# Retention and two mixture layers on one core: the first load of turned queries and keys as one transfer or as two

## The chip, the cores and the metric

The kernel runs on one core of one Trainium2 chip. The metric is the device time of one execution in microseconds, as the median of several runs. Besides these runs there is one profiled execution; all rows of the trace come from it.

## What is computed

Three stages follow one another. The first is a retention (a linear attention with a decaying state) over 2 batches, 8 heads, 768 positions and 64 numbers a head; the second is a dense layer of 512 to 2048 to 512 with a leaky rectifier; the third sends each of the 1536 tokens to one of 8 experts.

```python
def _attn_ref(q, k, v):                      # 2, 8, 768, 64
    gamma = 1.0 - 2.0 ** (-5.0 - np.arange(H))
    for t in range(S):
        state = gamma * state + np.einsum('bhd,bhe->bhde', k[:, :, t], v[:, :, t])
        y[:, :, t] = scale * np.einsum('bhd,bhde->bhe', q[:, :, t], state)

def _moe_ref(x, w_in, w_out):                # 1536 x 512, 512 x 2048, 2048 x 512
    h = x @ w_in
    return np.maximum(0.01 * h, h) @ w_out

def _moe2_ref(x, w_gate, w1, w2, capacity):  # 8 experts, 512 x 1024 and 1024 x 512
    expert_idx = np.argmax(x @ w_gate, axis=1)
    ...
    h = np.maximum(np.einsum('ecd,edf->ecf', disp, w1), 0.0)
    y = np.einsum('ecf,efd->ecd', h, w2)
    ...
```

## The kernel before

The retention is done in chunks of 128 positions, six to a batch, so twelve chunks, named 0 to b. The host lays each chunk out as 128 rows of 2048 numbers: 512 of turned queries (head dimension on the partitions, two heads one above the other, so four pairs of heads beside each other), 512 of turned keys in the same layout, 512 of keys and 512 of values as they are. One load, `q` and the chunk, takes the first 1024 numbers of every row, and another, `k` and the chunk, the last 1024. Each is 512 KB: 128 rows of 4 KB.

All loads go through one function, `issue` (L148), on SyncE's queue, in the order of the list `LOADS` (L35): q0, k0, q1, w00, k1, q2, k2, q3 and so on. The first six go into tiles named `early`, the later ones into tiles named `land`. After load 0 the decay masks of the retention are loaded (`cst`, columns from `C_D`, 512 KB), and after load 1 the factors of queries and keys (`cst`, columns from `C_GQ`, 286 KB). The rest of the constants (206 KB) and the small `wg_sb` follow after all loads that can be issued at once.

The order of the engines' work in the front part is written out by hand in the list `FRONT` (L40). What begins it is `S.0 am.00 am.01 M.0 ks.0 D.0 xh.0 st.0 xl.0 S.1 qs.1 Y.1 am.10 am.11 ...`:

- S (L183, matmuls of L190) is the scores of a chunk: eight products, four pairs of heads by two heads, of turned keys and turned queries, two of them for each pair. An fp32 product stands as two MATMUL rows in the trace, so S.0 is 16 rows. Its loop takes the pairs in order.
- am (L212, DVE) multiplies the scores of one half of the heads by the decay mask in `cst`.
- M (L256, PE) multiplies the masked scores by the values, which come with load `k`.
- ks (L198, DVE) multiplies the keys by factors in `cst`; D (L228, PE) sums keys and values into the state; st (ACT) copies the state.
- xh (L265, ACT) and xl (L269, DVE) write the chunk's output as a high and a low part. qs (L207, DVE) and Y (L245, PE) bring in the state of earlier chunks. Chunk 0 has no qs and no Y.
- c1 to c4 and A1, A2 split the weights of the dense layer into a high and a low part (L291 to L310, on DVE and ACT).

Ahead of S.0, PE does nine matmuls with zeros (L1024) and one that clears the state (L217), and behind S.0 27 small ones with zeros (L1076). They need no load.

Of the kernel before, what the change touches and what calls it, by code (L numbers as in the profile page):

```python
# [59 lines left out]
def retention_moe_moe_kernel(ctx: ExitStack, tc: tile.TileContext, qkv, wb, wc, wg, const, out, cap):  # L60
    nc = tc.nc
# [86 lines left out]
    def issue():  # L148
        while issued[0] < len(items):
            n = issued[0]  # L150
            if n >= EARLY + LAND and items[n - LAND] not in done:
                return
            key = items[n]
            issued[0] += 1
            pool, tag = (early_p, "early") if n < EARLY else (land_p, "land")
            t = pool.tile([P, 1024], U32 if key[0] == "w" else F32, tag=tag, name=tag)
            if key[0] == "w":
                src = wb[key[1], :, key[2] * 1024:(key[2] + 1) * 1024]
            elif key[0] == "u":
                src = wc[key[1] // PF // slabs, key[1] % PF]  # L160
            else:
                o = 0 if key[0] == "q" else 1024
                src = qkv[key[1] // NCH, key[1] % NCH, :, o:o + 1024]
            nc.sync.dma_start(out=t, in_=src)
            if n in (0, 1):
                first_const.pop(0)()
            landed[key] = t

    def used(key):
        done.add(key)  # L170
        issue()
# [818 lines left out]
    def out_tiles():  # L990
        return [c_p.tile([P, DM], F32, tag="og", name="og", bufs=4) for _ in range(BT)]
# [23 lines left out]
    with tc.manual_schedule():  # L1015
# [10 lines left out]
        first_const.append(lambda: load_const(C_D, C_D + 1024))  # L1026
        first_const.append(lambda: load_const(C_GQ, C_ID))
        issue()
        load_const(C_ID, NC)
        nc.sync.dma_start(out=wg_sb, in_=wg)  # L1030
# [29 lines left out]
        for n in names:  # L1060
            n, c = n.split(".")
# [4 lines left out]
        for n in names:  # L1066
            n, c = n.split(".")
# [112 lines left out]
        for t in range(BT):  # L1180
# [14 lines left out]
            out=xr0[0][:, 0, :], out_offset=None, in_=x2d,  # L1195
# [36 lines left out]
        for s in range(NS):  # L1232
            o = out_tiles()
            n, base = every[s // slabs], (s % slabs) * BW
# [76 lines left out]
```

## Time and profile before

| | us |
|---|---|
| runs without the profiler, median of 3 | 527.96 |
| lowest and highest of them | 527.80, 528.04 |
| profiled execution, its own time | 526.96 |
| its span, first to last instruction | 525.1 |
| PE busy in the span | 509.6 |

The profiled execution is 1.0 us below the median of the runs. Time in the rows is counted from the start of the span. PE is the matmul engine, PEld its weight loads, DVE, ACT and POOL the vector, scalar and general engines, SPq the sequencer of SyncE, which issues the loads. A timeline's line gives start, duration, engine, line of the kernel, operation, written and read tiles, how many instructions were merged (x16), and in brackets the idle time ahead of it with what ended that.

### The profile page before, as it was taken

The page shows a single profiled execution, that of the slowest core. Times are in us where ns is not written, and L with a number is a line of the kernel's source. Part 1 is how long each engine was busy: PE and PEld are TensorE (multiplying, and loading weights), DVE is VectorE, ACT ScalarE, POOL GpSimd, SP SyncE. Part 2 cuts the span into 40 slices and gives each one's busy share as a digit, 9 for nine tenths or more (in the row PEclk, how much of TensorE's full clock was granted, in tenths as well). Part 3 has the DMA queues.
Part 4 walks back from the last instruction along what each step waited for, and adds up shares of the span by engine and source line. Part 5 has one row for each costly group of instructions (what it writes and reads, how often), then busy time and mean ns, then how long its engine had stood idle before and what let it go on. Part 6 is the DMA issues. An engine that isn't in the chain of part 4 may idle for free.

```text
span 525.1 us, 9022 instructions
## 1 busy us (share of the span) xinstructions
PE 509.6 (97%) x3328; PEld 459.9 (88%) x3330; DVE 338.7 (64%) x670; ACT 253.2 (48%) x573; POOL 50.1 (10%) x75
## 2 busy tenths in 40 slices
PE   8899999999999999999999999999979999999994
PEld 5888989999999999999999999789779899999893
DVE  3999994279779848974742445667534466676560
ACT  2886964365555534432423224346433266676440
POOL 0000000000000000000100107334010031220101
PEclk9999999999999999999999999999979999999998
DMA  8987672022315702220200108589445099993001
GB/s 308 398 282 241 229 248 102 1 81 81 101 42 142 249 30 80 81 80 1 81 32 29 61 1 296 168 277 318 160 149 206 7 335 361 330 371 119 24 10 44
DMA packets 24940, 80.79 MB, mean 154 GB/s; under 512 B 3706, under 2 KB 3834, under 8 KB 24864
## 3 DMA queue, kind: packets, MB, share of 16 engines
q1 hardware_dynamic: 21312, 70.26, 38.4%
q0 software_dynamic: 3552, 9.58, 5.2%
q8 instruction: 40, 0.66, 0.5%
q14 instruction: 36, 0.29, 0.2%
HBM read 72.35 MB, written 9.96 MB: 157 GB/s over the span
## 4 chain that ended last, share of the span: by engine, by line
PE 68%; DMA 24%; DVE 3%; issue 2%; ACT 1%; POOL 0%; SPq 0%; POOLq 0%; ACTq 0%; DVEq 0%
PE ps_h L363 25%; PE ps_y L414 16%; DMA out<-og,gix 12%; DMA xr<-x2d,gix 8%; PE ps_a L414 7%; PE ps_h L826 5%; PE ps_y L878 5%; PE ps_a L256 2%; PE ps_a L190 2%; PE ps_a L245 1%; DMA xpre<-wc,wix 1%; DMA early<-qkv 1%; PE ps_a L463 1%; DMA land<-qkv 1%; PE ps_h L228 1%
## 5 line engine op out<-in xcount | busy, mean ns | idle before, releaser
L370 ACT ACTIVATE hs<-ps_h 128x384 f32<-128x384 f32 x64 | 31.4, 490 | 97.1 <-PE ps_h L363 97.1
L375 DVE SCALAR_TENSOR_TENSOR hs<-hs 128x384 f32<-128x384 f32 x64 | 35.6, 556 | 65.7 <-ACT hs L370 65.5
L363 PE MATMUL ps_h<-xh,hi 128*128 128x384 f32 x256 | 56.3, 341 | 0.0
L414 PE MATMUL ps_y<-hi,gh 128*128 128x512 f32 x138 | 56.3, 408 | 0.0
L363 PE MATMUL ps_h<-xh,lo 128*128 128x384 f32 x256 | 55.5, 338 | 0.0
L363 PE MATMUL ps_h<-xl,hi 128*128 128x384 f32 x256 | 55.5, 338 | 0.0
L379 ACT ACTIVATE gh<-hs 128x384 fp32r<-128x384 f32 x64 | 33.7, 526 | 43.2 <-DVE hs L375 43.2
L414 PE MATMUL ps_y<-hi,gl 128*128 128x512 f32 x138 | 53.9, 391 | 0.0
L414 PE MATMUL ps_y<-lo,gh 128*128 128x512 f32 x138 | 53.8, 390 | 0.0
L363 PEld LDWEIGHTS ps_h<-xh,hi 128*128 128x128 f32 x256 | 46.0, 188 | 4.8
L385 DVE TENSOR_TENSOR gl<-hs,gh 128x384 fp32r<-128x384 f32 x64 | 35.6, 556 | 21.3 <-ACT gh L379 21.3
L363 PEld LDWEIGHTS ps_h<-xl,hi 128*128 128x128 f32 x256 | 45.9, 187 | 0.0
L363 PEld LDWEIGHTS ps_h<-xh,lo 128*128 128x128 f32 x256 | 45.9, 187 | 0.0
L878 PE MATMUL ps_y<-hi,gh 128*128 128x512 f32 x104 | 41.1, 395 | 0.0
L878 PE MATMUL ps_y<-hi,gl 128*128 128x512 f32 x104 | 40.8, 392 | 0.0
L878 PE MATMUL ps_y<-lo,gh 128*128 128x512 f32 x104 | 40.8, 392 | 0.0
L869 DVE SCALAR_TENSOR_TENSOR gl<-ps_h,gh 128x256 fp32r<-128x256 f32 (+2 forms) x42 | 16.6, 395 | 33.4 <-ACT gh L868 33.4
L849 DVE TENSOR_TENSOR lo<-xland,hi 128x1024 fp32r<-128x1024 f32 (+1 forms) x32 | 33.5, 1056 | 7.2 <-ACT hi L848 7.1
L868 ACT ACTIVATE gh<-ps_h 128x256 fp32r<-128x256 f32 (+2 forms) x42 | 15.3, 364 | 40.5 <-PE ps_h L826 25.4
L849 DVE TENSOR_TENSOR lo<-land,hi 128x1024 fp32r<-128x1024 f32 (+1 forms) x30 | 31.0, 1043 | 5.0 <-ACT hi L848 5.0
L414 PEld LDWEIGHTS ps_y<-hi,gl 128*128 128x128 f32 x138 | 25.9, 188 | 5.6
L414 PEld LDWEIGHTS ps_y<-hi,gh 128*128 128x128 f32 x138 | 25.9, 188 | 4.1 <-issue 0.3
(201 smaller groups left out, 1011.3 us busy)
## 6 DMA issues: line engine op xcount, KB each, us to landing
land<-wc SPq DMA_DIRECT2D x32, 512.0 KB, 6.9
xland<-wc SPq DMA_DIRECT2D x32, 512.0 KB, 5.1
land<-wb SPq DMA_DIRECT2D x31, 512.0 KB, 4.9
land<-qkv SPq DMA_DIRECT2D x19, 512.0 KB, 5.3
out<-zero SPq DMA_DIRECT2D x12, 256.0 KB, 6.0
x2d<-rows SPq DMA_DIRECT2D x12, 256.0 KB, 2.1
early<-qkv SPq DMA_DIRECT2D x5, 512.0 KB, 7.3
cst<-cst_in SPq DMA_DIRECT2D x1, 512.0 KB, 5.6
```

The lines of the kernel that those rows point to most:

```text
L190: nc.tensor.matmul(out=at["s", c][h2][:, a, :], lhsT=kT[r, a, :], rhs=qT[r, a, :], start=True, stop=True)
L363: nc.tensor.matmul(out=h_ps, lhsT=w[i][:, dc * P:(dc + 1) * P], rhs=x[j][:, dc, :], start=(n == 0), stop=(n == 3 * KD - 1))
L370: nc.scalar.activation(out=hs, in_=gt[u][0], func=ACTF.Copy)
L375: nc.vector.scalar_tensor_tensor(out=hs, in0=hs, scalar=0.01, in1=hs, op0=ALU.mult, op1=ALU.max)
L379: nc.scalar.activation(out=gh, in_=gt[u][0], func=ACTF.Copy)
L385: nc.vector.tensor_tensor(out=gl, in0=hs, in1=gh.bitcast(F32), op=ALU.subtract)
L414: nc.tensor.matmul(out=yb[ti][t], lhsT=gt[u][i][:, t * P:(t + 1) * P], rhs=w[j][:, 512:1024], start=(f == fs[0] and n == 0), stop=(f == fs ...
L826: r = nc.tensor.matmul(out=hp, lhsT=w[i][:, dc * P:(dc + 1) * P], rhs=(h, l)[j][:, dc, 0:cls * P], start=(n == 0), stop=(n == 3 * KD - 1))
L849: nc.vector.tensor_tensor(out=lo[:, o], in0=src[:, o], in1=hi[:, o].bitcast(F32), op=ALU.subtract)
L868: nc.scalar.activation(out=gh, in_=hp, func=ACTF.Relu)
L869: nc.vector.scalar_tensor_tensor(out=gl, in0=hp, scalar=0.0, in1=gh.bitcast(F32), op0=ALU.max, op1=ALU.subtract)
L878: nc.tensor.matmul(out=yps[t], lhsT=gg[i][:, t * P:(t + 1) * P], rhs=w[j][:, 512:1024], start=(k == 0 and n == 0), stop=(k == PF - 1 and n ...
```

## The change

Load 0 (q0) is issued as two transfers in place of one. Tile and source are seen as 128 rows of two halves (queries and keys) of 512 numbers; the first transfer takes the first 256 numbers of both halves, which are pairs 0 and 1 of queries and keys, the second the last 256, pairs 2 and 3. Each moves 256 KB in pieces of 1 KB, where the one before moved 512 KB in pieces of 4 KB. Everything else stands as it was; the masks are issued behind the second transfer.

```diff
@@ -161,7 +161,12 @@
             else:
                 o = 0 if key[0] == "q" else 1024
                 src = qkv[key[1] // NCH, key[1] % NCH, :, o:o + 1024]
-            nc.sync.dma_start(out=t, in_=src)
+            if n == 0:
+                by = [x.rearrange("p (m w) -> p m w", m=2) for x in (t, src)]
+                for o in (slice(0, 256), slice(256, 512)):
+                    nc.sync.dma_start(out=by[0][:, :, o], in_=by[1][:, :, o])
+            else:
+                nc.sync.dma_start(out=t, in_=src)
             if n in (0, 1):
                 first_const.pop(0)()
             landed[key] = t
```

## Rows read from the trace of the kernel before

**Rows 1.** The page: busy time by engine, and the chain that ended last.
```profile
PE 509.6 (97%) x3328; PEld 459.9 (88%) x3330; DVE 338.7 (64%) x670; ACT 253.2 (48%) x573; POOL 50.1 (10%) x75
...
PE 68%; DMA 24%; DVE 3%; issue 2%; ACT 1%; POOL 0%; SPq 0%; POOLq 0%; ACTq 0%; DVEq 0%
```

**Rows 2.** Windows: length, busy time of PE, PEld, DVE, ACT, POOL, PEclk, DMA, GB/s.
```profile
1.50:3.00 1.50, 1.50 (x5) 0.57 (x4) 0.00 (x0) 0.72 (x2) 0.31 (x4) 1.00 0.75 147
3.00:4.50 1.50, 1.50 (x5) 0.46 (x4) 0.00 (x0) 0.00 (x0) 0.00 (x0) 1.00 0.94 281
...
12.00:15.00 3.00, 2.81 (x44) 2.35 (x44) 3.00 (x7) 1.50 (x3) 0.00 (x0) 1.00 1.03 418
20.00:500.00 480.00, 474.25 (x3028) 431.77 (x3029) 318.37 (x636) 238.73 (x543) 47.27 (x64) 0.99 0.44 153
```

**Rows 3.** Timeline of PE over the first 12 us.
```profile
1.19 4.02 PE L1024 MATMUL ps_y<-zero 128*128 128x512 bf16 x9 [1.19 <-DVE zero L1019]
5.00 0.63 PE L217 MATMUL ps_h<-zero 128*128 128x512 bf16 x1
5.56 1.55 PE L190 MATMUL ps_a<-early 64*128 64x128 f32 x16
...
8.18 1.40 PE L256 MATMUL ps_a<-am,early 128*64 128x128 f32 x16 [0.18 <-DMA early<-qkv]
9.63 0.69 PE L228 MATMUL ps_h<-early,ks 128*64 128x64 f32 x16
10.31 1.16 PE L190 MATMUL ps_a<-early 64*128 64x128 f32 x16
```

**Rows 4.** Timeline of PE in two narrow windows, 6.7:7.0 and 8.6:9.6.
```profile
6.50 0.61 PE L190 MATMUL ps_a<-early 64*128 64x128 f32 x8
...
8.49 1.09 PE L256 MATMUL ps_a<-am,early 128*64 128x128 f32 x14
```

**Rows 5.** Timeline of DVE from 7 to 13 us.
```profile
7.15 1.29 DVE L212 TENSOR_TENSOR am<-ps_a,cst 128x512 f32<-128x512 f32 x2 [6.02 <-PE ps_a L190]
8.89 0.69 DVE L198 TENSOR_TENSOR ks<-early,cst 128x512 f32<-128x512 f32 x1 [0.45 <-DMA cst<-cst_in]
10.24 0.69 DVE L269 TENSOR_TENSOR xl<-ps_a,xh 128x512 fp32r<-128x512 f32 x1 [0.67 <-ACT xh L265]
10.85 0.68 DVE L207 TENSOR_TENSOR qs<-early,cst 128x512 f32<-128x512 f32 x1
11.47 1.29 DVE L212 TENSOR_TENSOR am<-ps_a,cst 128x512 f32<-128x512 f32 x2
```

**Rows 6.** Timeline of SyncE's queue; the 12.72 line is from a narrow window.
```profile
0.73 0.38 SPq L164 DMA_DIRECT2D early<-qkv  x1
1.17 0.42 SPq L1017 DMA_DIRECT2D cst<-cst_in  x1
...
5.26 1.86 SPq L164 DMA_DIRECT2D land<-qkv  x2
8.06 0.33 SPq L164 DMA_DIRECT2D land<-wb  x1
8.81 0.33 SPq L164 DMA_DIRECT2D land<-qkv  x1
10.19 0.33 SPq L164 DMA_DIRECT2D land<-wb  x1
...
12.72 0.33 SPq L164 DMA_DIRECT2D land<-qkv  x1
14.00 0.33 SPq L1017 DMA_DIRECT2D cst<-cst_in  x1
```

**Rows 7.** Issues at 0.73, 12.72 and 14.00: KB, us from issue to landing.
```profile
early<-qkv SPq DMA_DIRECT2D x1, 512.0 KB, 4.5
...
land<-qkv SPq DMA_DIRECT2D x1, 512.0 KB, 11.2
...
cst<-cst_in SPq DMA_DIRECT2D x1, 206.0 KB, 10.4
```

## The prediction

> **What bounds the kernel now.** I read the page first. PE is busy for 509.6 of 525.1 us and holds 68% of the chain that ended last [rows 1]; in the windows it is busy for 474.25 of the 480 us from 20 to 500 [rows 2]. So from 20 us on the end is set by PE, and a change in the first 12 us is worth what it moves the start of that stretch by, one for one, and no more. The question is only how many tenths of a microsecond the front moves, and which way.
>
> Then the front, event by event. The timeline of SyncE tells when loads land: eight transfers can be under way, the ninth issue starts at 5.26, right after q0 landed at 0.73 + 4.5 = 5.24 [rows 6, 7], and each later one stands just behind a landing. So the starts of rows 6 are landings: q0 5.24, masks (the second of the two issues, 5.26 + 1.86 - 0.33) 6.79, k0 8.06, factors 8.81, q1 10.19. 512 KB land 1.27 us apart (6.79 to 8.06). The loads are one stream, and an issue that is queued costs nothing by itself.
>
> PE has the zero matmuls in front of S.0: ten of them at (5.00 - 1.19) / 9 = 0.42 us each, the last from 5.00, so PE is free at about 5.43 [rows 3]. S.0 starts at 5.56 because q0 landed at 5.24; some 0.3 us lie between the landing and the first matmul. From there the chain is: S.0 ends at 7.11; am.00 and am.01 run from 7.15 to 8.44 [rows 5]; M.0 starts at 8.18, held by k0, but its third instruction, at 8.49, needs am.01, and the last 14 end at 9.58 [rows 3, 4]. Beside it ks.0 waits for the factors and runs from 8.89 to 9.58 [rows 5], so D.0 starts at 9.63, ends at 10.32, and S.1 follows at 10.31, just after q1 (10.19) [rows 3, 6]. S.1's scores and the DVE queue (xl.0, qs.1) reach am.10 together at 11.47 [rows 5]; from then on DVE is full (3.00 of 3.00 us from 12 to 15 [rows 2]). In this stretch three loads arrive just when they are wanted: k0, the factors, q1.
>
> **The change part by part.**
>
> *The first half lands earlier.* S.0's pairs 0 and 1 need 256 KB in place of 512. That can be worth at most the wait that PE has now, 5.56 - 5.43 = **0.13 us**, because ahead of S.0 PE is busy with zeros. The first half of S.0 then takes the 0.8 us or so from 5.43 to 6.2 that it takes now (the last eight of 16 rows start at 6.50, 0.94 after the first [rows 4]), and the second half of the load, which would land at 5.24 plus what the split costs, is there in time unless the split costs more than about 0.7 us. So S.0 ends 0.06 to 0.13 us sooner: nearer 0.06, since PE goes from a slow to a double pace within S.0 (eight rows in 0.94 us, then eight in 0.61 [rows 4]) and a start that is earlier may only add slow time.
>
> *What that is worth to the end.* am.00 could follow S.0 at 7.02 to 7.09 if the masks are there (6.79 now). am.01 and M.0's last 14 follow. But M.0's start hangs on k0: unstalled it needs about 1.33 us from its start (0.24 for two instructions and 1.09), so from 8.18 it ends at 9.51 at best. D.0 hangs on ks.0, which hangs on the factors, and does not move at all. Gain on the xl.0 path: at most 0.07 us; on the D.0, S.1, am.10 path: none.
>
> *Pieces of 1 KB in place of 4 KB.* q0 becomes 512 pieces in place of 128. No row shows a piece of 1 KB, so I bound it by other sizes. 16 engines share 128 rows, eight each. 4096 B: 1.27 / 8 = 159 ns a piece. 2288 B (factors): 8.81 - 8.06 = 0.75, so 94 ns. 1648 B (last constants): landed at 14.00 + 10.4 = 24.4, behind a load that landed at 12.72 + 11.2 = 23.9, so 0.5 us and about 65 ns, known to 0.1 us only [rows 6, 7]. The straight line through the first and the second gives 49 ns for 1024 B, through the first and the third 42 ns. A row's 4 KB then costs 168 to 196 ns in place of 159, and eight of them 0.08 to 0.29 us more. A harder reading charges the factors with all that came late up to q1: 10.19 - 8.06 - 1.27 = 0.86 us, 107 ns, a line that gives 71 ns for 1024 B and eight times 4 x 71 - 159, about **1.0 us**. That is my upper end; the lower end is nothing, if the slow start of the stream hides it. I take **0.2 us**, from the two straight lines, because the 1648 B piece is nearest in size and was measured in an undisturbed stream.
>
> The Trainium skill (DMA: Bandwidth & Descriptors, "Why small descriptors are slow (HBM only)") counts some three cycles a packet beside one for each 32 bytes; by that four packets of 1 KB cost 140 cycles for 131, an estimate of 0.09 us here. It is the low side of what the rows give.
>
> *Where this goes.* All loads behind q0 land 0.2 us later, since the stream has no hole: masks 6.99, k0 8.26, factors 9.01, q1 10.39. The masks now arrive together with the scores and eat the gain of S.0. M.0 then ends at 8.18 + 0.2 + 1.33 = 9.71 in place of 9.58; ks.0 ends at 9.78; D.0, S.1 and am.10 follow 0.2 us late. DVE and then PE carry that to the end: **+0.2 us**.
>
> *One more issue on SyncE.* Issues at the start are 0.44 apart (0.73 to 1.17 [rows 6]), so masks, k0 and what follows are issued that much later. They queue behind q0, which keeps the stream busy until 5.24; covered, at 0.44 us if it were not. With eight transfers under way, q2 becomes the ninth and waits for the first half of q0; it lands near 14 us, some nine us after its issue, so that is hidden as well, and behind it every load waits for the same landing as before. PE gets one more wait, on an instruction that it has anyway.
>
> Sum, on the profiled execution: 526.96 + 0.2 = 527.16. The runs' median stands 1.00 above it, so **528.15 us**, rounded down to 528.1.
>
> **The rivals.**
>
> *Nothing moves, or a hair of gain.* The stream is slow at first: 147 and 281 GB/s in the two windows from 1.5 to 4.5, against 418 from 12 to 15 [rows 2]. If what slows it there hides the cost of a piece, the loads land as now, S.0 gains its 0.06 to 0.13, and the chain 0 to 0.07: 527.9. The opening stretch speaks for it, the straight lines against.
>
> *Slower by over 0.2%.* The slow start is paid by the piece. From 1.5 to 4.5 the stream moved 1.5 x 147 + 1.5 x 281 = 642 KB; at 418 GB/s that is 1.54 us, so 1.46 us were lost over 642,000 / 4096 = 157 pieces, 9.3 ns each. q0 has 384 pieces more: +3.6 us, 531.5. It decides from 1.06 / 384 = 2.8 ns a piece on. Its place is masks, k0 and factors, which all land late, and a hole in S.0 between its halves. Such a hole might also put off the pace change of PE that comes within S.0; M.0, D.0 and S.1 (1.09 + 0.69 + 1.16 [rows 3, 4]) at half pace are up to 2.9 us more. Against it: a slow start at engines that had nothing to do before is more likely paid once. The Trainium skill (the same page, "Anatomy of one DMA") gives about 2 us fixed for each DMA on its software path; paid one after the other, that would put q0's second half far behind. Landings of queued loads 1.27 and 0.75 us apart [rows 6] speak against that here.
>
> *The halves are not seen as halves.* If S.0's first matmul waits for both transfers, it starts at 5.24 + 0.2 + 0.3, some 0.2 later than now. S.0 then ends at about 7.3, am.01 at 8.6, M.0 at 9.75, while D.0 goes by the factors as above: the same +0.2, so it would show in the trace and hardly in the time.
>
> *Faster by over 0.2%.* Even a stream that ran 1.4 us ahead would leave S.0 behind the zeros, at 5.43; the gain stays at 0.13. What is left is something later that no row of the front shows.
>
> **How the numbers follow.** About 0.2%, 1.06 us, is what a measurement of this kernel can tell from no change. Forecast (+0.1 to +1.0, with both readings of the halves): 0.61. Nothing or a hair: 0.19. Slower by over 0.2%: 0.14. Faster by over 0.2%: 0.06. The predicted time is the forecast's. The range goes from 527.5, under the second case by the scatter of the runs, to 529.3, past the upper end for the pieces (527.96 + 1.0) into the slow case. Faster 0.06, same 0.80, slower 0.14.
>
> **What would show it.** Right: S.0 starts near 5.43 with its first eight rows, without a hole; issues behind landings stand 0.1 to 0.3 us later (k0 near 8.26, factors near 9.01); ks.0 and am.10 start 0.2 us late; the PE stretch from 20 us on has the length that it has now. Wrong: k0 and the factors land at 8.06 and 8.81 (no cost of a piece) or past 9 and 10 (cost by the piece in the slow start); a hole within S.0; PE's pace changing after S.0; or a difference of a microsecond or more that arises behind 20 us.

## The result, and the profile after

The changed kernel is slower. Its median is **533.08 us** (529.30 to 534.80, nine runs) against 527.96 us, a ratio of 1.0072 (95% interval 1.0047 to 1.0096). Two later comparisons on other chips gave 1.0018 (0.9992 to 1.0043) and 1.0056 (1.0024 to 1.0087): the direction is the same each time, the size is not, and the reason for that is part of what follows. The profiled execution took 533.08 us, its span is 531.3 us: 6.2 us longer than before.

The time is lost in two places, one in the first 12 us and one near 345 us. First the front. The timeline of SyncE's queue, to be read as [rows 6]: each issue stands just behind the landing that lets it go.

```profile
6.10 2.21 SPq L169 DMA_DIRECT2D land<-qkv  x2
9.27 0.33 SPq L169 DMA_DIRECT2D land<-wb  x1
10.58 0.33 SPq L169 DMA_DIRECT2D land<-qkv  x1
11.82 0.33 SPq L169 DMA_DIRECT2D land<-wb  x1
```

Masks land at 6.10 + 2.21 - 0.33 = 7.98 (before 6.79), k0 at 9.26 (8.06), the factors at 10.57 (8.81). Yet the halves of q0 are early: by the events of their semaphores they landed at 3.74 and 4.43, where the whole came at 5.24. So the pieces that were cut small came fast, and what comes behind them is late. A load counts as landed when the last of the 16 DMA engines is done with its rows, and the masks show what that means: 15 engines were done with them by 6.88 (6.61 before), the last only at 7.97 (6.78 before).

The timelines of PE and DVE say what that does, beside [rows 3] and [rows 5] (the changed kernel's lines stand five lower from L164 on, so L190 is now L195):

```profile
5.56 1.71 PE L195 MATMUL ps_a<-early 64*128 64x128 f32 x16
7.20 0.96 PE L1081 MATMUL ps_y<-zero 128*32 128x64 bf16 x27
9.39 1.10 PE L261 MATMUL ps_a<-am,early 128*64 128x128 f32 x16 [1.23 <-DVE am L217]
11.40 0.69 PE L233 MATMUL ps_h<-early,ks 128*64 128x64 f32 x16 [0.91 <-DVE ks L203]
12.02 1.16 PE L195 MATMUL ps_a<-early 64*128 64x128 f32 x16
...
24.80 1.05 PE L250 MATMUL ps_a<-qs,st 128*128 128x128 f32 x8
```

```profile
8.07 1.29 DVE L217 TENSOR_TENSOR am<-ps_a,cst 128x512 f32<-128x512 f32 x2 [6.94 <-DMA cst<-cst_in]
10.66 0.69 DVE L203 TENSOR_TENSOR ks<-early,cst 128x512 f32<-128x512 f32 x1 [1.30 <-DMA cst<-cst_in]
...
13.21 1.29 DVE L217 TENSOR_TENSOR am<-ps_a,cst 128x512 f32<-128x512 f32 x2 [0.66 <-PE ps_a L195]
```

S.0 starts at 5.56, as before, in one piece without a hole. Then each step waits for a load where before it waited for at most 0.45 us: am.00 for the masks (DMA in the bracket; before, it was PE that ended the wait), M.0 until 0.13 after k0 (the bracket names am.01, which ended at about the same time), ks.0 until 0.09 after the factors. S.1 starts at 12.02 in place of 10.31 (+1.71), am.10 at 13.21 in place of 11.47. At 24.80 the product of L250 is 1.74 late (at 23.06 before), at 47 us the same instructions are 2.04 late.

The windows show the stream and the hole on PE, with the columns of [rows 2]. The changed kernel, then the kernel before:

```profile
1.50:3.00 1.50, 1.50 (x5) 0.57 (x4) 0.00 (x0) 0.72 (x2) 0.31 (x4) 1.00 0.64 178
3.00:4.50 1.50, 1.50 (x5) 0.46 (x4) 0.00 (x0) 0.00 (x0) 0.00 (x0) 1.00 1.12 294
4.50:6.00 1.50, 1.50 (x7) 0.59 (x7) 0.00 (x0) 0.00 (x0) 0.00 (x0) 1.00 0.81 265
6.00:8.00 2.00, 2.00 (x43) 1.88 (x41) 0.00 (x0) 0.00 (x0) 0.00 (x0) 1.00 1.00 306
8.00:10.00 2.00, 0.77 (x17) 0.67 (x15) 1.29 (x2) 0.00 (x0) 0.00 (x0) 1.00 0.99 354
...
341.00:348.00 7.00, 7.00 (x45) 6.38 (x43) 1.92 (x8) 1.16 (x4) 1.45 (x3) 0.52 0.47 128
```

```profile
4.50:6.00 1.50, 1.50 (x7) 0.58 (x7) 0.00 (x0) 0.00 (x0) 0.00 (x0) 1.00 0.97 352
6.00:8.00 2.00, 2.00 (x43) 1.76 (x41) 0.85 (x2) 0.00 (x0) 0.00 (x0) 1.00 0.98 386
8.00:10.00 2.00, 1.77 (x29) 1.41 (x30) 1.13 (x2) 0.39 (x1) 0.00 (x0) 1.00 1.01 391
...
341.00:348.00 7.00, 6.90 (x66) 6.15 (x64) 4.63 (x26) 1.75 (x6) 1.80 (x4) 1.00 0.81 247
```

In the first 4.5 us the stream is a little faster than before (178 and 294 GB/s against 147 and 281). From 4.5 to 6 us it moves 265 GB/s against 352, with the DMA engines less busy (0.81 against 0.97). From 6 to 8 us it moves 306 against 386 at about the same busy share: there they are as busy, with slower pieces. PE is busy for 0.77 us of the 2 us from 8 to 10, where it was busy for 1.77.

The second place is in the last row of each: from 341 to 348 PE's granted clock is 0.52 in this execution and 1.00 before. The timelines of PE there, after and before:

```profile
341.19 1.86 PE L709 MATMUL ps_h<-xt,xpre 128*128 128x128 f32 x8
342.85 1.72 PE L468 MATMUL ps_a<-wg_sb,xt 128*128 128x8 f32 x8
344.42 2.05 PE L709 MATMUL ps_h<-xt,xpre 128*128 128x128 f32 x8
...
347.96 1.19 PE L709 MATMUL ps_h<-xt,xpre 128*128 128x128 f32 x8
```

```profile
339.00 1.06 PE L704 MATMUL ps_h<-xt,xpre 128*128 128x128 f32 x8
339.89 0.96 PE L463 MATMUL ps_a<-wg_sb,xt 128*128 128x8 f32 x8
340.71 1.14 PE L704 MATMUL ps_h<-xt,xpre 128*128 128x128 f32 x8
...
342.72 1.14 PE L704 MATMUL ps_h<-xt,xpre 128*128 128x128 f32 x8
```

Row against row the changed kernel is late by 2.19, 2.96, 3.71 and 5.24 us: the same eight products take 2.05 us in place of 1.14, which is the lower clock level (1.2 in place of 2.4 GHz). So of 6.2 us, 1.74 come from the front, 0.45 more by 339 us, 3.05 from this fall of the clock; another 1.0 net comes later, where the clock falls once more in both kernels (0.62 granted from 380 to 388 before, 0.57 from 388 to 396 after). The 0.45 need no cause in the change: in a second profile of the kernel before, S.1 starts at 10.30, and the rows at 339 us are 0.69 later than in the first.

That fall is not in every execution. The profile of the same changed kernel on a third chip (529.50 us, span 527.7) has the late front and no fall here; the same three rows:

```profile
340.89 1.06 PE L709 MATMUL ps_h<-xt,xpre 128*128 128x128 f32 x8
341.79 0.96 PE L468 MATMUL ps_a<-wg_sb,xt 128*128 128x8 f32 x8
342.60 1.14 PE L709 MATMUL ps_h<-xt,xpre 128*128 128x128 f32 x8
```

They are 1.89 us late, no more than the front explains. As each run's record has its mean granted clock, the runs can be split by it; 0.989 lies between their clusters. A run under it has a further fall somewhere; the mean doesn't say where.

| | runs | clock under 0.989 | median of these | median of the others |
|---|---|---|---|---|
| changed kernel, all three chips | 31 | 16 | 532.97 | 529.50 |
| kernel before, beside the experiments | 112 | 22 | 531.36 | 528.55 |

The others differ by 0.95 us, which is less than the front's loss of 1.7; the rest of the difference in the median is that half of the runs of the changed kernel have a further fall of the clock (7 of 9, 3 of 10 and 6 of 12 on the three chips), against a fifth before.

### The profile page after: what moved, and what is told of

Same layout as the page of the kernel before. It is cut to its first block, busy times and chain, and to the rows that moved or that the text cites. A ratio compares the mean times of both kernels' runs of the same rounds, so it can differ in the third digit from the quotient of the medians.

```text
span 531.3 us, 9023 instructions
## 1 busy us (share of the span) xinstructions
PE 513.3 (97%) x3328; PEld 463.5 (87%) x3330; DVE 339.0 (64%) x670; ACT 252.9 (48%) x573; POOL 50.4 (9%) x75
## 2 busy tenths in 40 slices
DMA packets 25340, 80.79 MB, mean 152 GB/s; under 512 B 3722, under 2 KB 4362, under 8 KB 25264
## 4 chain that ended last, share of the span: by engine, by line
PE 71%; DMA 18%; issue 4%; DVE 3%; ACT 2%; another core or an unknown queue 1%; POOL 1%; SPq 0%; POOLq 0%; ACTq 0%; DVEq 0%
PE ps_h L368 24%; PE ps_y L419 16%; DMA out<-og,gix 9%; PE ps_a L419 7%; DMA xr<-x2d,gix 7%; PE ps_y L883 5%; PE ps_h L831 5%; PE ps_a L261 2%; PE ps_a L195 2%; PE ps_h L709 2%; PE ps_a L250 2%; PE ps_a L468 2%; DMA cst<-cst_in 1%; DMA xpre<-wc,wix 1%; PE ps_y L720 1%
```

## The experiments

**Is it chance?** The kernel before and the changed one again, as they are, on another chip.

> The kernel before, unchanged, for a second profile and the granted clock of each run. The shown profile has the masks at 6.78, the factors at 8.79, S.1 at 10.31, and PE at half clock from 381.9 to 388.7 and in the last microseconds, not between 330 and 350. Theory 'pieces' (the split makes the stream late): masks and factors within 0.2 us of these. Theory 'chance' (the slow start of the stream differs from execution to execution, whatever the kernel): masks anywhere from 6.7 to 8.0. Theory 'phase' (the late half of the loss is PE's clock, which falls or not according to where a stretch with idle PE lies): runs mostly at a mean clock of 0.990 and near 528; a run above 531 has a clock below 0.987.

> The changed kernel, unchanged, for a second profile. Its first one has q0's halves at 3.74 and 4.43, masks 7.97, k0 9.26, factors 10.57, S.1 at 12.02 (1.71 late), and half clock from 341.2 to 348.1 as well, which the kernel before has not there. 'Pieces': masks at 7.6 to 8.3, S.1 1.4 to 2.0 us late again. 'Chance': S.1 anywhere between 0 and 2 us late. 'Phase': a run whose mean clock is 0.985 or less is above 532, one with 0.990 or more below 532.

Measured: 0.9988 (0.9964 to 1.0013) and 1.0018 (0.9992 to 1.0043); medians 528.05 and 530.68. The front repeats to two tenths of a microsecond: masks 6.82, k0 8.09, factors 8.83, S.1 10.30 in the first; masks 8.15, k0 9.44, factors 10.56, S.1 12.21 in the second. The late front belongs to the change. The interval of the time does not exclude no difference on this chip. The profile of the second shows another fall, in the front; two windows and PE's row of S.1:

```profile
8.00:10.00 2.00, 0.42 (x8) 0.46 (x10) 1.29 (x2) 0.00 (x0) 0.00 (x0) 1.00 0.96 337
11.80:15.10 3.30, 3.30 (x30) 2.96 (x27) 1.62 (x4) 0.60 (x1) 0.00 (x0) 0.50 1.03 422
```

```profile
5.27 1.16 PE L195 MATMUL ps_a<-early 64*128 64x128 f32 x16
...
12.21 2.08 PE L195 MATMUL ps_a<-early 64*128 64x128 f32 x16
```

Here PE had reached its full pace before S.0, so it was done with S.0 and the zeros sooner, the hole ahead of M.0 was longer (busy 0.42 of 2 us), and S.1 ran at half the clock: 2.08 us in place of 1.16. Near 345 us the clock does not fall in this execution, so its mean of 0.988 comes from the front.

**Is it two transfers, or their pieces?** Two transfers of the first load again, with larger pieces: by columns (all queries, then all keys: pieces of 2 KB), and by rows (64 rows each: pieces of 4 KB).

```diff
 if n == 0:
-    by = [x.rearrange("p (m w) -> p m w", m=2) for x in (t, src)]
-    for o in (slice(0, 256), slice(256, 512)):
-        nc.sync.dma_start(out=by[0][:, :, o], in_=by[1][:, :, o])
+    for o in (slice(0, 512), slice(512, 1024)):            # two_2k
+        nc.sync.dma_start(out=t[:, o], in_=src[:, o])
+    for r in (slice(0, 64), slice(64, 128)):               # two_4k
+        nc.sync.dma_start(out=t[r, :], in_=src[r, :])
```

> q0 as two transfers, queries and keys, in 256 pieces of 2 KB in place of 512 of 1 KB; one more issue, as in the change. 'Pieces': a part of the delay, masks at 7.1 to 7.6, S.1 0.5 to 1.2 us late. 'One more transfer' (the second issue ahead of the masks is what costs): the same as the change, S.1 1.5 to 2.0 late. 'Chance': no relation.

> q0 as two transfers of 64 rows each, in the 128 pieces of 4 KB of the kernel before; one more issue, as in the change. 'Pieces': no delay, masks at 6.7 to 7.0, S.1 within 0.3 us of 10.31, total near 528. 'One more transfer': S.1 1.5 to 2.0 us late, total near 532. 'Chance': no relation.

Measured: 1.0001 (0.9975 to 1.0026) and 1.0016 (0.9992 to 1.0040). SyncE's queue and S.1, first with 2 KB, then with half the rows:

```profile
5.45 1.58 SPq L168 DMA_DIRECT2D land<-qkv  x2
7.95 0.33 SPq L168 DMA_DIRECT2D land<-wb  x1
8.83 0.33 SPq L168 DMA_DIRECT2D land<-qkv  x1
...
10.31 1.16 PE L194 MATMUL ps_a<-early 64*128 64x128 f32 x16
```

```profile
6.09 1.36 SPq L168 DMA_DIRECT2D land<-qkv  x2
8.40 0.33 SPq L168 DMA_DIRECT2D land<-wb  x1
9.49 0.33 SPq L168 DMA_DIRECT2D land<-qkv  x1
...
10.93 1.16 PE L194 MATMUL ps_a<-early 64*128 64x128 f32 x16
```

With 2 KB pieces masks (6.68), k0, factors and S.1 are where they were before. So a second transfer with its issue costs nothing, as the prediction had it. Half the rows in each transfer cost 0.8 us at q0 itself (its second half lands at 6.08), 0.3 at masks and k0 and 0.6 at S.1: the size of the piece is not all there is.

**Is it the form of the transfer, or the number of short pieces?** Four plain transfers of 256 columns, pieces of 1 KB, none with queries and keys together; and the change with the masks in two transfers of 2 KB pieces.

```diff
 if n == 0:
+    for o in (0, 512, 256, 768):                           # four_1k
+        nc.sync.dma_start(out=t[:, o:o + 256], in_=src[:, o:o + 256])
```
```diff
-first_const.append(lambda: load_const(C_D, C_D + 1024))    # after_m2k
+first_const.append(lambda: [load_const(c, c + 512) for c in (C_D, C_D + 512)])
```

> q0 as four transfers of 128 KB, one piece of 1 KB a row each: the 512 pieces of the change, without its pattern of two pieces a row, and two more issues than the change. 'Pieces of 1 KB': masks at 7.6 to 8.4, factors 9.8 to 10.8, S.1 1.2 to 2.2 us late. 'Pattern' (two pieces a row with a jump between them are what costs): masks under 7.2, S.1 under 0.6 us late.

> The change, with the masks as two transfers of 2 KB pieces behind it. If the 4 KB pieces that come first behind short ones pay the slow start (they took up to 2 us each in the changed kernel, where those of q0 took 46 ns), 2 KB pieces soften it: both mask transfers landed by 7.3, factors by 9.4, S.1 less than 0.7 us late. If the short pieces leave the 16 engines out of step, whatever follows: masks near 8, factors 10 or later, S.1 1.4 us late or more.

Measured: 1.0037 (1.0019 to 1.0055) and 1.0019 (0.9992 to 1.0045). With four transfers k0 lands at 9.10, the factors at 10.63, S.1 starts at 12.09: from k0 on the change's front again, without its pattern of two pieces a row. Its beginning differs, and fits neither of the two expectations: q0's last quarter lands at 5.90, later than the whole did before, and the masks at 7.15, only 0.37 late. What the two further issues add is not tested apart. With the masks in 2 KB pieces these land at 6.23 and 6.87, as early as before, k0 at 8.91 and the factors at 9.73; S.1 starts at 11.35, and runs at half the clock (2.08 us). This lies between the two expectations. So the load behind the short pieces is slow when it comes in 4 KB pieces; of what is saved there, 1.1 us, k0, the next load in 4 KB pieces, keeps 0.35.

**Does a short piece cost that anywhere?** The same split on the sixth load, q2, which is under way at 13 us.

```diff
-if n == 0:
+if n == 5:                                                 # mid_1k
```

> The two transfers of 1 KB pieces are those of load 5 (q2) in place of load 0, where the stream runs at its full pace and nobody waits for the next load. If short pieces throw the stream back wherever they stand: the landings behind q2 are 1.2 us or more later than in the kernel before (k2 at 15.26 there, q3 16.53). If they do so only in the slow start of the stream: k2 and q3 0.1 to 0.5 us later, the price of the pieces themselves, with masks, k0 and factors as in the kernel before.

There is one profiled execution and no runs beside it. The front is as before (masks 6.71, factors 8.77, S.1 10.22). The queue of SyncE, beside its issues at 12.72 and 14.00 in [rows 6]:

```profile
12.69 1.08 SPq L169 DMA_DIRECT2D land<-qkv  x2
14.14 0.33 SPq L1022 DMA_DIRECT2D cst<-cst_in  x1
15.40 0.33 SPq L1035 DMA_DIRECT2D wg_sb<-wg  x1
```

By the issues behind them, q2 landed 0.14 us later than before and k2 0.12 (15.28 before). That is within the 0.08 to 0.29 us of the straight lines. Inside the stream the price of 512 short pieces is what was predicted; at its start what they cost the loads behind them is about ten times that. (The time, 531.90, is that of an execution with a mean clock of 0.985, and says nothing of this.)

**Does it help if the masks go ahead?** The masks first, then the split load.

```diff
 if n == 0:
+    first_const.pop(0)()                                   # masks_first
 ...
-if n in (0, 1):
+if n == 1:
     first_const.pop(0)()
```

> The change with the masks issued ahead of the two transfers of q0 in place of behind them, so that the stream starts with 4 KB pieces and the short ones come second. If the slow start is paid by whichever 4 KB pieces come first, and the short ones only passed it on to loads that are waited for: masks near 5.2 (as q0 in the kernel before), q0's second half near 6.9, k0 by 8.5, factors by 9.2, S.1 within 0.6 us of 10.31. If short pieces within the first microseconds disturb what follows by themselves: k0 past 9, factors past 10, S.1 1.2 us late or more, as in the change.

Measured: 0.9989 (0.9957 to 1.0021), no run of ten under 0.989, though the kernel before had five of 13 so in that comparison; the runs over 0.989 have medians of 528.56 and 527.32. Masks land at 4.38, the halves of q0 at 5.54 and 6.72, k0 at 9.38, the factors at 10.29. The masks, at the head of the stream in 4 KB pieces, were whole 0.86 us sooner than q0 at the head was before (5.24) and than was expected of them (5.2); why is not shown. PE:

```profile
6.76 0.71 PE L196 MATMUL ps_a<-early 64*128 64x128 f32 x8 [0.47 <-DMA early<-qkv]
...
9.52 1.09 PE L262 MATMUL ps_a<-am,early 128*64 128x128 f32 x16 [1.15 <-DMA early<-qkv]
...
11.74 1.16 PE L196 MATMUL ps_a<-early 64*128 64x128 f32 x16
```

Here S.0 has its hole between the halves, so the halves are seen as halves. k0, now the load behind the short pieces, is 1.3 us late even though they are not the first in the stream. What they disturb is what follows them within the first microseconds, whichever load that is.

**Does a late front without short pieces cost the same?** Five zero matmuls more ahead of S.0; and the factors issued behind q1 in place of k0.

```diff
-for i in range(9):
+for i in range(14):                                        # late_5
```
```diff
-if n in (0, 1):
+if n in (0, 2):                                            # fact_late
```

> The kernel before with 14 zero matmuls ahead of S.0 in place of 9: PE starts S.0 about 2 us later, the loads stay as they were (masks near 6.8, factors near 8.8), and S.1 comes some 1.5 us late, as far as the change puts it. Theory 'phase' (a front that is late by 1.5 us moves the stretch near 335 us, where PE waits much, against the times at which the clock can fall, or gives it more often): more runs with a mean clock under 0.989 than the 8 of 41 of the kernel before, 4 or more in 10, and their median 2.5 to 3.5 us above the others. Theory 'lottery' (the clock falls in a fifth of the executions whatever the front does, and the first nine runs of the change were unlucky): about 2 in 10, and the other runs 1.5 us above those of the kernel before.

> The kernel before with the factors loaded behind q1 in place of ahead of it: no piece and no transfer more, but the factors land near 10.1 in place of 8.8, so ks.0, D.0 and S.1 come about 1.3 us late, with the same empty stretch on PE in front of D.0 as in the change. The landings from w00 on stay where they were (11.4 and on). If what the change costs is the late factors and nothing else, its runs with an undisturbed clock (0.989 or more) are 1.2 to 1.8 us above those of the kernel before. 'Phase' (a late front with an empty PE makes the clock fall more often): 4 or more in 10 of its runs under 0.989. 'Lottery': 2 in 10, as in the kernel before.

The first missed its aim. S.0 starts at 6.75, 1.2 us late, but S.1 at 10.76, only 0.45 late: S.0 ran at full pace (1.16 us in place of 1.55), and the 0.45 us for which DVE waited for the factors before [rows 5] are used up (ks.0 starts at 9.14, right behind am.01); am.10 is 0.77 late (12.24). Measured 1.0034 (1.0010 to 1.0058), two of twelve runs under 0.989; runs over it: 529.99 against 528.84.

The second moves the factors' landing to 10.79 and S.1 to 12.68, with no piece of a load under 2288 B. Measured: 1.0052 (1.0031 to 1.0074), eight of twelve runs under 0.989, as slow as the change. PE's rows and its windows in the two places:

```profile
11.63 1.12 PE L228 MATMUL ps_h<-early,ks 128*64 128x64 f32 x16 [2.45 <-DVE ks L198]
...
11.80:15.10 3.30, 3.30 (x34) 2.96 (x35) 1.28 (x3) 0.60 (x1) 0.00 (x0) 0.50 1.03 421
341.00:348.00 7.00, 7.00 (x53) 6.60 (x52) 2.67 (x10) 1.16 (x4) 1.44 (x3) 0.76 0.35 103
```

So late factors alone, without short pieces, give a hole of 2.45 us on PE, the lower clock from 10.97 on, within that hole, and a time like the change's. The small pieces are the cause of the late loads, and a late load alone can bring the rest. For the fall near 345 it is not needed, though: the profiles of two_2k and mid_1k, whose S.1 starts at 10.31 and 10.22, have it as well.

```profile
341.00:348.00 7.00, 7.00 (x47) 6.28 (x47) 2.97 (x17) 1.05 (x4) 1.44 (x3) 0.66 0.51 153
341.00:348.00 7.00, 7.00 (x46) 6.33 (x45) 2.54 (x14) 0.95 (x4) 1.45 (x3) 0.60 0.48 150
```

The first row is two_2k's, the second mid_1k's (clock 0.66 and 0.60).

**The changed kernel once more, and a version that might beat both.** The split in 2 KB pieces, with the 30 KB of factors that hold those of ks.0 (60 columns) sent ahead of the other 256 KB, and q1 between them.

```diff
-if n in (0, 1):
+if n in (0, 1, 2):                                         # small_first
     first_const.pop(0)()
...
-first_const.append(lambda: load_const(C_GQ, C_ID))
+first_const.append(lambda: load_const(C_GS, C_ID))
+first_const.append(lambda: load_const(C_GQ, C_GS))
```

> The changed kernel beside it, on the same chip. Its undisturbed runs 1.2 to 1.8 us above those of the kernel before; 'phase': half of the runs under a mean clock of 0.989; 'lottery': 2 in 10, and the whole difference to the kernel before about 0.3% in place of the 0.7% of the first comparison. Factors at 10.3 to 10.8 again.

> A candidate: q0 as two transfers of 2 KB pieces (queries, keys), and of the factors the 60 columns that ks.0 needs behind k0, the 512 that qs.1 needs behind q1. ks.0 then waits for 30 KB in place of 286, and q1 lands about 0.6 us sooner. D.0 starts near 9.3, S.1 near 9.9, 0.3 to 0.6 us sooner than in the kernel before. In the time that is under what can be measured, so within 0.2% of the kernel before; if a sooner front also spares clock falls, up to 0.3% below.

The changed kernel: 1.0056 (1.0024 to 1.0087), six of twelve runs under 0.989. The other: S.1 at 10.05, 0.26 sooner than before, and 0.9989 (0.9967 to 1.0010), no run of ten under 0.989. That is within what the measurement can tell from no change; it doesn't beat the kernel before. The trace says where the 0.26 us go: xl.0 waits for xh.0 and starts at 10.32 (10.24 before), qs.1 and am.10 follow on DVE, and am.10 starts at 11.53, where it started at 11.47.

## Why the prediction was wrong

*The price of a short piece was right, in a stream that runs.* 42 to 49 ns from the straight lines; the trace's DMA records give 46 ns as the median of the changed q0's pieces, and the 0.12 to 0.14 us of mid_1k are the 0.2 us of the sum within its bounds. (The line to 42 starts from 65 ns, where 0.5 / 8 is 62.5; by that it gives 38, and a lower bound of nothing in place of 0.08. And 527.16 + 1.00 is 528.16.)

*The step that failed is "All loads behind q0 land 0.2 us later, since the stream has no hole."* Masks came 1.2 us late, k0 1.2, the factors 1.8. The stream's pieces of 4 KB change their pace: of the 248 that begin between 5.3 and 9.5 us, 59 take over 200 ns, against 16 of 323 before; most take 159 ns as before, and one that begins at 4.42 takes 2047. And the engines get out of step: k0's ends on the 16 of them are spread over 2.1 us in place of 1.2. By 12.7 us 3406 KB (of 1024 bytes) have been moved in place of 3722; at 418 GB/s [rows 2] that is 0.77 us, and the rest of the delay is the spread: with q1, the middle engine is 0.75 us late, the last 1.62. The masks' delay is all spread, since their middle engine was done at the same time as before (6.1). The sum treated "the stream" as one pipe with a rate, and a landing as the point at which its bytes are through.

*The waits were read right.* M.0 hangs on k0 (0.12 behind it before, 0.13 after), ks.0 on the factors (0.08 and 0.09), D.0, S.1 and am.10 follow them: with the measured landings the working of the prediction gives S.1 as it came. It was the landings that were wrong.

*The gain of S.0 was not there.* "The wait that PE has now, 5.56 - 5.43" was read as a wait for q0, with "some 0.3 us" between the landing and the first matmul. With the first half at 3.74, S.0 still started at 5.56. Where PE does wait for the load, the traces put that gap at 0.04 to 0.13 us (landing and start: 6.72 and 6.76 in masks_first, 5.14 and 5.18 in fact_late, 5.24 and 5.37 in two_2k). S.0's start in the kernel before went by PE's pace: S.0 follows the start of the clearing product by 0.56 us at the slow pace (5.00 and 5.56 in either kernel, whether the load landed at 5.24 or at 3.74) and, with the load there, by 0.31 at the full one (4.96 and 5.27 in again_after). So the 0.13 us were no wait for a load.

*"One for one, and no more" failed too.* Medians moved by 1.8 to 5.1 us for 1.7 us at the front. One for one isn't shown even for the runs over 0.989: they moved by less (0.95 us pooled; 1.16 and 1.09 on the two later chips), and if runs of the same mean clock are compared, by 1.68 at 0.990 (8 against 28) and by 0.58 at 0.993 (4 against 27). And a hole in the front can cost clock there: behind idle stretches of 2.12, 2.25 and 2.45 us (after_m2k, again_after, fact_late) S.1 ran at half the clock, which is 0.9 us for S.1 itself in again_after; in the other profiles with a late front it did not. Last, more runs of the changed kernel have a further fall.

The rival for slower had the sign and the place (masks, k0 and factors late), with 0.14, but not its mechanism: it had the short pieces pay the slow start themselves, +3.6 us and a hole in S.0. They did not; q0 was whole 0.8 us sooner. The 4 KB pieces behind them paid, with 1.7 us at the front. That its 531.5 lies among the measured medians (530.68 to 533.08) is luck: its 3.6 us were to arise in the front, which lost 1.7, and a fall of the clock near 345 was not in it. The doubt that the rival raised, PE's pace put off, was right in kind: what a hole costs in clock was worth a term of its own.

**What stays open.** Why pieces of 4 KB are slow behind shorter ones in the first 9 us and not at 13: the experiments place it, none explains it. Nor is it settled what brings on the further fall of the clock. A fifth of the runs of the kernel before have one, and two_2k and mid_1k show one near 345 behind a front that is not late. Runs with one are more frequent with S.1 late by 1.7 or more (the change, four_1k with five of ten, fact_late with eight of twelve), but masks_first has S.1 1.43 late and no such run in ten. A link to how the front's holes lie is only argued.

## What to carry to other kernels

A load that is split to be used sooner should be split so that its pieces stay long, above all where the first loads of a kernel are queued behind it: look at the landings of the loads behind it, not only at its own. Price a piece where it will be, since the price in a running stream says little of the first microseconds. And where PE is the bound, a wait in the front is not only its length: read the granted clock behind it, and compare runs by their mean clock before a median is taken for the effect of an edit. Where the clock fell, only a profile of that execution can say.

## What the runs showed of the hardware that was not expected

- 512 pieces of 1 KB in two transfers at the start of the stream came through 0.8 us sooner than 128 of 4 KB (4.43 against 5.24), and made the loads behind them 1.2 to 1.8 us late. In four transfers they came through at 5.90. Pieces of 2 KB did neither: the second half landed at 5.24, the factors at 8.81.
- Splitting 128 rows into 64 and 64, with pieces of 4 KB, delayed the loads behind by 0.3 to 0.7 us.
- The median durations of a piece are 46 ns for 1024 B, 84 for 2048, 93 for 2288 and 159 for 4096 (the change, two_2k, the kernel before). They lie on one line: by estimate 8 ns for each piece and 27 bytes a nanosecond on each of the 16 engines.
- PE's change of pace at the start comes at another point in each execution: S.0's 16 rows took 1.16, 1.55, 1.71 or 1.88 us in the first two profiles of either kernel, with the same zeros ahead. The Trainium skill (TensorE: Matmul & The Clock Gate, "What's actually happening") says that the check of activity is free-running and doesn't start anew with the kernel, so that the point varies; these four durations agree.
- A mean granted clock of 0.985 in place of 0.990 in a run goes with some 3 us in 530; a mean under 0.989 comes in a fifth of the runs of an unchanged kernel, and in nine or ten runs its share can look like the effect of an edit.
